# Loads of w_out in pieces of 64 columns, kept in that order on chip, and another room for its fifth load

## The chip, the cores and the metric

The kernel runs on one core of one Trainium2 chip. The metric is the device time of one execution in microseconds (us); lower is better. TensorE does the matrix products, VectorE (DVE), ScalarE (ACT) and GpSimd (POOL) the elementwise work, and SyncE (SP) mostly issues transfers. Each engine works through a queue of its own in order; transfers issued by SP and by ACT run on the same 16 DMA engines.

## The reference

Attention with a causal mask and a bias from a running sum, on 8 batches of 8 heads, 576 positions and 64 values per head, followed by a gated feed-forward layer on the 4608 x 512 result:

```python
scores = scale * np.matmul(q, k.transpose(0, 1, 3, 2))
cum = np.cumsum(np.maximum(s, 0.0), axis=-1)
bias = -(cum[:, :, :, None] - cum[:, :, None, :])
scores = np.where(causal, -1e9, scores + np.minimum(bias, 0.0))
attn = softmax(scores)                       # exp(scores - max) / sum
x = np.matmul(attn, v)                       # 8,8,576,64 -> 4608 x 512
gate = 1.0 / (1.0 + np.exp(-(x @ w_gate)))   # 512 x 1536
out = (gate * (x @ w_val)) @ w_out           # 1536 x 512
```

q, k, v, s are float32; the three weights are float64.

## The kernel before

**Precision.** Operands of the large products are split into a high and a low float16 part, and three products (high x high, high x low, low x high) are summed. The float64 weights arrive as pairs of 32-bit words and are turned into float32 on the chip (`decode_weight`: one ACT pass, line 270, and three DVE passes, lines 271 to 273), then scaled and split (`split_weight`: ACT at lines 286 and 291, a sum over partitions on POOL at line 288, DVE at line 292).

**Weight steps.** There are 18 steps, worked through by `weight_step` in order. Steps 0 to 11 bring a block of 128 columns of w_gate and w_val each. Steps 12 to 17 bring 256 rows of w_out each, 1 MB of float64 (two row blocks f and f+1 of 128 rows; a partition gets one row of each, 8 KB). `room(n)` names the place where the raw words of step n land (`raw`), the place of its float32 values (`dec`), and the step that must have been worked before the load may be issued. For the six w_out steps these stand in `outroom`. All six share the one float32 place `dec[0]` (tile `wa`). `raw[0]` is tile `ws`; `raw[1]` to `raw[3]` lie in the still unused parts of `w2all`; `raw[4]` and `raw[5]` lie in `t2big` (tile `t2f`), which later holds intermediate results of feed-forward units 8 to 15 and 16 to 23. At the start of step n, `weight_step` issues each outstanding load whose last step is below n. The loads of steps 12 and 13 are issued apart from that, at ticks 22 and 30 of the main loop. So the fifth w_out load (step 16) is issued at the start of step 15 into the room of step 14, and the sixth (step 17) at the start of step 17 into the room of step 16.

**Transfers of w_out.** `load_weight` splits a w_out load into two transfers on ACT's queue (lines 251 and 258), by halves of the 512 columns: 256 columns of both row blocks each, which are runs of 256 float64 (2 KB). `w2all[:, f]` then holds the 512 columns of the high part of row block f in one run, and those of the low part after it.

**Attention.** The first 8 heads (batch 0) are computed in float32; from head 8 on q, k and the probabilities are split into float16 parts and turned round by transposing transfers on SP's queue: `T<-qk` (line 394), `pt<-p` (line 493), `x<-x` (line 528). `swap_k` copies between partition halves (`T<-T`, lines 399 and 400) so that the second product of each score (line 446) can follow the first (line 445). `load_qk` (line 346) brings q and k of two heads in runs of 64 float32.

**Feed-forward.** The 4608 rows are cut into groups of 256. A unit (g, f) is one group and one of the 12 blocks of 128 hidden columns. `ffn_in` does 24 products with 256 columns each (line 656), `ffn_out` three per 128 rows with 512 columns of w_out as the moving operand (line 686, 1296 in all). The 24 units of the first two groups keep their result in `t2first` until all weight steps are done: `hidden_scale` needs the scales of all of them, and only after it do the products of line 686 begin. Weight steps 13 to 17 are emitted ahead of unit 12. A scheduler orders each engine's queue by priority with a simulated timeline.

Of the kernel before, what the change touches and what calls it, by code (L numbers as in the profile page):

```python
# [7 lines left out]
F16 = mybir.dt.float16  # L8
F32 = mybir.dt.float32
F32R = mybir.dt.float32r  # L10
I32 = mybir.dt.int32
# [5 lines left out]
P = 128  # L17
# [6 lines left out]
def tile_attention_then_gated_ffn(  # L24
# [13 lines left out]
    NT, DM = out.shape  # L38
# [4 lines left out]
    NF = DFF // P  # L43
# [13 lines left out]
    cp = ctx.enter_context(tc.tile_pool(name="cp", bufs=1))  # L57
# [10 lines left out]


    w1 = [cp.tile([P, NC, 2, 2, P], F16, name=f"w1_{f}") for f in range(NF)]  # L70
    w2all = cp.tile([P, NF, 2, DM], F16, name="w2all")
    w2 = [w2all[:, f] for f in range(NF)]
    e_s = [cp.tile([P, n * P], F32, name=f"e_{i}") for i, (_, _, n) in enumerate(SETS)]
    p_s = [cp.tile([P, 2, n * P], F16, name=f"p16_{i}") for i, (_, _, n) in enumerate(SETS)]

# [45 lines left out]
    def pow2_of(dst, ss, tag):  # L121

        e = wp.tile([P, 1], I32, tag="xe", name=f"xe_{tag}")
        nc.vector.tensor_scalar(e, ss.bitcast(I32), 1, 0x3F800000, ALU.logical_shift_right, ALU.bitwise_and)
        n = dst.shape[1]
        nc.vector.tensor_scalar(dst.bitcast(I32), e.to_broadcast([P, n]) if n > 1 else e, -1.0, 204.0 * 2.0 ** 23,
                                ALU.mult, ALU.add)
# [83 lines left out]

    raw0 = lp.tile([P, 8 * P, 2], I32, name="ws0")
    dec0 = lp.tile([P, 8 * P], I32, name="wa0")
    flat = w2all.rearrange("p f l n -> p (f l n)").bitcast(I32)
    raw = [raw0] + [flat[:, i * 16 * P : (i + 1) * 16 * P].rearrange("p (n t) -> p n t", t=2) for i in range(2)]
    dec = [dec0] + [flat[:, i * 8 * P : (i + 1) * 8 * P] for i in range(4, 6)]

# [3 lines left out]

    for i in (1, 2):
        raw.append(t2big[:, 8 * i * GT : 8 * (i + 1) * GT].bitcast(I32).rearrange("p (n t) -> p n t", t=2))
    outroom = [(4, 0, 0), (5, 0, 0), (0, 0, NF - 3), (3, 0, NF - 1), (0, 0, NF + 2), (0, 0, NF + 4)]

    def room(n):

        o, f = wsteps[n]
        if o == 0:
            return raw[f % 3], dec[f % 3], n - 3  # L230
        i, j, last = outroom[f // 2]
        return raw[i], dec[j], last

    def load_weight(n):
        o, f = wsteps[n]
        fs = slice(f * P, (f + 1) * P)
        r, d, _ = room(n)
        for x, src in enumerate((w_out,) if o else (w_gate, w_val)):
            src = src[f * P : (f + 2) * P, :] if o else src[:, fs]
            if wide:  # L240
                src = src.bitcast(I32)
                dst = r.rearrange("p n t -> p (n t)")
            else:
                dst = d.bitcast(F32)
            if o == 0:
                src = src.rearrange("(c p) n -> p c n", p=P)
                dst = dst.rearrange("p (c x n) -> p c x n", c=NC, x=2)[:, :, x]
            else:
                src = src.rearrange("(x p) (h n) -> h p x n", p=P, h=2)
                dst = dst.rearrange("p (x h n) -> h p x n", x=2, h=2)  # L250
                ins = nc.scalar.dma_start(dst[0], src[0])
                if n < NF + 2:
                    tc.keep_in_program_order(ins)
                src, dst = src[1], dst[1]
            if n < 2:
                nc.sync.dma_start(dst, src)
            else:
                ins = nc.scalar.dma_start(dst, src)
                if n == 2 or NF <= n < NF + 2:
                    tc.keep_in_program_order(ins)  # L260

    def decode_weight(n):

        o, f = wsteps[n]
        r, a, _ = room(n)
        if not wide:
            return a.bitcast(F32)
        m = w2all[:, f : f + 2].rearrange("p f l n -> p (f l n)") if o else w1[f].rearrange("p c g l n -> p (c g l n)")
        m = m.bitcast(I32)
        nc.scalar.activation(a.bitcast(F32), r[:, :, 1].bitcast(F32), AF.Copy, scale=2.0 ** -112)  # L270
        nc.vector.tensor_scalar(m, a, 3, 0x7FFFFFF8, ALU.logical_shift_left, ALU.bitwise_and)
        nc.vector.scalar_tensor_tensor(a, a, -0x80000000, m, ALU.bitwise_and, ALU.bitwise_or)
        nc.vector.scalar_tensor_tensor(a, r[:, :, 0], 29, a, ALU.logical_shift_right, ALU.bitwise_or)
        return a.bitcast(F32)

    def split_weight(n, a):

        o, f = wsteps[n]
        if o:
            a = a.rearrange("p (x n) -> p x n", x=2)  # L280
            hi, lo = w2all[:, f : f + 2, 0], w2all[:, f : f + 2, 1]
        else:
            a = a.rearrange("p (c n) -> p c n", n=P)
            hi, lo = (w1[f].rearrange("p c g l n -> p (c g) l n")[:, :, l] for l in range(2))
        ss = wp.tile([P, 1], F32, tag="wss", name=f"wss{n}")
        nc.scalar.activation(hi, a, AF.Square, accum_out=ss)
        tot = wp.tile([P, 1], F32, tag="wst", name=f"wtot{n}")
        nc.gpsimd.partition_all_reduce(tot, ss, P, ADD_REDUCE)
        pow2_of(wscale[:, o, f : f + 1 + o], tot, f"w{n}")
        sc = wscale[:, o, f : f + 1]  # L290
        nc.scalar.activation(hi, a, AF.Copy, scale=sc)
        nc.vector.scalar_tensor_tensor(lo, a, sc, hi, ALU.mult, ALU.subtract)
# [26 lines left out]
    def weight_step():  # L319
        n = wnext["step"]  # L320
        while n and wnext["load"] < len(wsteps) and room(wnext["load"])[2] < n:
            if not NF <= wnext["load"] < NF + 2:
                load_weight(wnext["load"])
            wnext["load"] += 1
        split_weight(n, decode_weight(n))
        wnext["step"] = n + 1
# [387 lines left out]
    for wnext["load"] in range(2):  # L714
        load_weight(wnext["load"])
# [13 lines left out]
    for n in range(nticks + 12):  # L729
# [13 lines left out]
        if 2 <= n < nticks + 2:  # L743
            a, z = divmod(n - 2, NTL)
# [5 lines left out]
        if 1 <= n < nticks + 1:  # L750
            a, z = divmod(n - 1, NTL)
# [7 lines left out]
        if 3 <= n < 3 + NTL * NN:  # L759
            with first():  # L760
                a, z = divmod(n - 3, NTL)
# [11 lines left out]
        if i < NH:  # L773
            p, j = divmod(i, 2)
            b, h = divmod(i, H)
# [80 lines left out]
            elif b == 1:  # L856
                if VSQ <= n < VSQ + vch:
                    v_square(2, n - VSQ)
                if VSQ + 5 <= n < VSQ + 5 + vch:
                    c = VSQ + 4 + vch - n  # L860
# [10 lines left out]
            if n in OUT:  # L871
                load_weight(NF + OUT.index(n))
# [3 lines left out]
        if n >= NE and state["u"] < 2 * NF:  # L876
            fdone = min(NF, int((n - NE + 1) * FPT))
            while state["u"] < 2 * fdone:
                f = state["u"]
# [17 lines left out]
        m = n - (11 if n > 2 * NTL * H + 30 else 7)  # L897
# [40 lines left out]
```

## Time and profile before

| | |
|---|---|
| runs | 1159.92, 1164.59, 1169.75 us (median 1164.59) |
| profiled execution | 1161.21 us, span 1159.4 us |
| mean granted TensorE clock | 0.979 |
| PE, PEld, DVE, ACT, POOL busy | 94%, 74%, 67%, 65%, 23% of the span |
| DMA queue of SP (q1) | 418398 packets, 127.12 MB |
| DMA queue of ACT (q10) | 13824 packets, 16.78 MB |

PE is the matrix product, PEld the loading of its stationary operand. Busy time of PE is counted from pipelined instructions, so a PE shown busy is not at its peak. A wait is put down to the event that came last. Names with an arrow are read as destination and source.

### The profile page before, as it was taken

How to read it: one execution, taken by the hardware profiler on the slowest of the kernel's cores; microseconds unless marked ns; L12 is line 12 of the kernel's file. 1: busy time of each engine (PE TensorE's matmuls, PEld its weight loads, DVE VectorE, ACT ScalarE, POOL GpSimd, SP SyncE). 2: the span in 40 equal slices, each digit the busy share in tenths (PEclk: the TensorE clock that was granted, in tenths of full speed). 3: DMA queues.
4: the chain of work that ended last, by engine and by line, in shares of the span. 5: the costliest groups of instructions: out<-in, count | busy, mean ns of one | idle time of the engine just before them, and what ended most of it. 6: DMA issues, size and time to landing. Idle time of an engine off the chain costs nothing.

```text
span 1159.4 us, 30337 instructions
## 1 busy us (share of the span) xinstructions
PE 1095.0 (94%) x11644; PEld 855.9 (74%) x11644; DVE 775.0 (67%) x2393; ACT 749.2 (65%) x1465; POOL 264.9 (23%) x570
## 2 busy tenths in 40 slices
PE   6786789989999999999999999999999999999997
PEld 5664677656777887778777777778877887787775
DVE  6888879785788777776566577777777775222221
ACT  6988667776777877676656577667777764233222
POOL 5535333231222222121111122222222221000000
PEclk9879899999999999999999999999999999999999
DMA  9675678898889797886737578877877764000000
GB/s 276 199 223 141 129 152 167 177 186 160 154 164 193 151 187 157 153 160 115 164 66 150 99 159 167 168 152 164 154 160 145 146 122 88 12 20 19 1 19 19
DMA packets 435886, 157.62 MB, mean 136 GB/s; under 512 B 403551, under 2 KB 423007, under 8 KB 435742
## 3 DMA queue, kind: packets, MB, share of 16 engines
q1 hardware_dynamic: 418398, 127.12, 57.1%
q10 hardware_dynamic: 13824, 16.78, 4.6%
q0 software_dynamic: 3520, 11.80, 3.1%
q8 instruction: 91, 1.49, 0.5%
q14 instruction: 53, 0.43, 0.1%
HBM read 56.92 MB, written 9.58 MB: 57 GB/s over the span
## 4 chain that ended last, share of the span: by engine, by line
PE 60%; issue 23%; DMA 5%; DVE 4%; ACT 3%; POOL 3%; SPq 1%; ACTq 0%; POOLq 0%; DVEq 0%
PE gv L656 33%; PE o L686 16%; PE s L446 3%; PE s L445 3%; DMA pt<-p 1%; PE av L505 1%; PE av L507 1%; PE av L506 1%; DMA T<-T 1%; POOL rl L460 1%; DMA T<-qk 1%; POOL cr L460 1%; PE na_ps L604 1%; DVE e L470 1%; DMA nqk<-in_q_dram 1%
## 5 line engine op out<-in xcount | busy, mean ns | idle before, releaser
L656 PE MATMUL gv<-x,w 128*128 128x256 f16 (+3 forms) x6912 | 614.9, 247 | 3.9 <-DVE t2f L663 2.3
L656 PEld LDWEIGHTS <-w 128*128 128x128 f16 x6912 | 535.1, 98 | 61.4 <-issue 4.6
L686 PE MATMUL o<-w2all,h 128*128 128x512 f16 x1296 | 314.8, 379 | 0.0
L460 POOL TENSOR_SCALAR_AFFINE_SELECT rl<-rl 128x64 f32<-128x64 f32 (+1 forms) x280 | 113.7, 407 | 512.0 <-DVE em L470 453.3
L473 ACT ACTIVATE e<-e,em 128x576 f32<-128x576 f32 x280 | 154.4, 554 | 88.0 <-DVE em L470 85.9
L661 ACT ACTIVATE th<-gv,scb 128x256 f32<-128x256 f32 (+3 forms) x288 | 111.3, 411 | 147.5 <-PE gv L656 142.5
L686 PEld LDWEIGHTS <-h 128*128 128x128 f16 x1296 | 123.4, 98 | 106.4
L663 DVE SCALAR_TENSOR_TENSOR t<-th,gv 128x256 f32<-128x256 f32 x192 | 80.0, 417 | 133.1 <-ACT th L661 131.9
L470 DVE CUSTOM_DVE_ANT_0 e<-s,rl,qkcf 128x288 f32<-128x288 f32 x280 | 135.7, 485 | 32.1 <-PE s L446 27.8
L671 ACT ACTIVATE h<-t,hsc 128x256 f16<-128x256 f32 x192 | 96.6, 503 | 80.4 <-DVE t L663 80.3
L482 DVE SCALAR_TENSOR_TENSOR p<-e,p 128x384 f16<-128x384 f32 x224 | 102.6, 498 | 41.0 <-ACT p L477 40.2
L672 DVE SCALAR_TENSOR_TENSOR h<-t,hsc,h 128x256 f16<-128x256 f32 x192 | 93.3, 486 | 43.4 <-ACT h L671 42.6
L477 ACT ACTIVATE p<-e 128x1152 f16<-128x1152 f32 x112 | 112.0, 1000 | 2.5
L505 PE MATMUL av<-v,pt 128*128 128x65 f16 x560 | 67.8, 193 | 5.3 <-DMA pt<-p 5.3
L446 PE MATMUL s<-T 128*128 128x288 f16 (+2 forms) x246 | 62.1, 279 | 11.3 <-DMA T<-T 11.3
L445 PE MATMUL s<-T 128*128 128x288 f16 (+2 forms) x246 | 64.4, 279 | 7.1 <-DMA T<-qk 4.2
L694 POOL DMA_DIRECT2D out_dram<-osb x36 | 20.4, 566 | 211.5 <-ACT osb L693 210.9
L507 PE MATMUL av<-v,pt 128*128 128x65 f16 x560 | 67.8, 194 | 0.0
L506 PE MATMUL av<-v,pt 128*128 128x64 f16 x560 | 67.7, 192 | 0.0
L505 PEld LDWEIGHTS <-pt 128*128 128x128 f16 x560 | 52.5, 98 | 11.0 <-DMA pt<-p 6.1
L408 POOL PARTITION_BROADCAST cr<-cr x63 | 58.5, 929 | 2.1 <-DMA cr<-cum_d 2.0
L506 PEld LDWEIGHTS <-pt 128*128 128x128 f16 x560 | 52.5, 97 | 4.9
(155 smaller groups left out, 1415.0 us busy)
## 6 DMA issues: line engine op xcount, KB each, us to landing
out_dram<-osb POOLq DMA_DIRECT2D x36, 256.0 KB, 2.8
v<-v SPq DMA_DIRECT2D x56, 162.5 KB
v<-in_v_dram SPq DMA_DIRECT2D x64, 128.0 KB
T<-T SPq DMA_DIRECT2D x82, 72.0 KB
t2f<-in_v_dram SPq DMA_DIRECT2D x20, 288.0 KB
qk<-in_q_dram SPq DMA_DIRECT2D x17, 288.0 KB
qk<-in_k_dram SPq DMA_DIRECT2D x17, 288.0 KB
w2all<-in_moe_w_gate_dram ACTq DMA_DIRECT2D x7, 512.0 KB
```

Source lines behind the costliest of these rows:

```text
L445: nc.tensor.matmul(ps[:, : b_ - a], lhs, T[i][:, 0, a:b_], start=True, stop=False)
L446: nc.tensor.matmul(ps[:, : b_ - a], lhs, T[i][:, 2, a:b_], start=False, stop=True)
L460: nc.gpsimd.affine_select(rl[i][:, q0:w], rl[i][:, q0:w], pattern=[[-1, m]], compare_op=ALU.is_ge, fill=-MASKED if i < NN else MASKED, bas ...
L470: nc.vector.tensor_tensor_reduce(e_t[t][:, a:b_], ps[:, : b_ - a], rl[i][:, a:b_], c, init, ALU.add, ALU.min, acc)
L473: nc.scalar.activation(e_t[t][:, :w], e_t[t][:, :w], AF.Exp, bias=init, scale=-1.0)
L477: nc.scalar.activation(p_s[h_][:, 0], e_s[h_], AF.Copy, scale=PSCALE)
L482: nc.vector.scalar_tensor_tensor(flat[:, LOW[t] * P : (LOW[t] + t) * P], e_t[t][:, : t * P], PSCALE, flat[:, kb * P : (kb + t) * P], ALU.m ...
L505: nc.tensor.matmul(AV[i][:, t], hi, v_[:, D : 2 * D + 1], start=kb == 0, stop=False)
L506: nc.tensor.matmul(AV[i][:, t, 0:D], hi, v_[:, 0:D], start=False, stop=False)
L656: nc.tensor.matmul(ps[:, gv, a:e], w1[f][:, cc, gv, wl], x_of(b, cc)[:, xl, c0 + a : c0 + e], start=(c == 0), stop=(c == 3 * NC - 1))
L661: nc.scalar.activation(th[:, a:e], ps[:, 0, a:e], AF.Tanh, scale=scb[b][:, f : f + 1])
L686: nc.tensor.matmul(ps[:m], h[:, hl, tt * P : tt * P + m], w2[f][:, wl], start=(f == 0 and c == 0), stop=(f == NF - 1 and c == 2))
```

## The change

It has two parts. First, a w_out load is split into its two transfers by row blocks instead of column halves, and each transfer is cut into pieces of 64 columns (512 bytes of float64), so that on chip the two row blocks alternate in pieces of 64 columns. That order is kept through decoding and splitting: `w2all` gets the shape [128, 6, 2, 8, 2, 64] (pair of blocks, high or low, piece, row block, column), and the moving operand of line 686 is read as 8 runs of 64 float16 (128 bytes) that lie 256 bytes apart. The bytes that each step occupies stay the same. Second, step 16 lands in `raw[5]` (the room of step 13) once step 13 has been worked, and step 17 in `raw[0]` once step 14 has been worked.

```diff
-    w2all = cp.tile([P, NF, 2, DM], F16, name="w2all")
-    w2 = [w2all[:, f] for f in range(NF)]
+    w2all = cp.tile([P, NF // 2, 2, 8, 2, DM // 8], F16, name="w2all")
+    w2 = [w2all[:, f // 2, :, :, f % 2] for f in range(NF)]
...
-    flat = w2all.rearrange("p f l n -> p (f l n)").bitcast(I32)
+    flat = w2all.rearrange("p f l h x n -> p (f l h x n)").bitcast(I32)
...
-    outroom = [(4, 0, 0), (5, 0, 0), (0, 0, NF - 3), (3, 0, NF - 1), (0, 0, NF + 2), (0, 0, NF + 4)]
+    outroom = [(4, 0, 0), (5, 0, 0), (0, 0, NF - 3), (3, 0, NF - 1), (5, 0, NF + 1), (0, 0, NF + 2)]
...
             else:
-                src = src.rearrange("(x p) (h n) -> h p x n", p=P, h=2)
-                dst = dst.rearrange("p (x h n) -> h p x n", x=2, h=2)
+                src = src.rearrange("(x p) (h n) -> x p h n", p=P, h=8)
+                dst = dst.rearrange("p (h x n) -> x p h n", x=2, h=8)
                 ins = nc.scalar.dma_start(dst[0], src[0])
...
-        m = w2all[:, f : f + 2].rearrange("p f l n -> p (f l n)") if o else w1[f].rearrange("p c g l n -> p (c g l n)")
+        m = w2all[:, f // 2].rearrange("p l h x n -> p (l h x n)") if o else w1[f].rearrange("p c g l n -> p (c g l n)")
...
         if o:
-            a = a.rearrange("p (x n) -> p x n", x=2)
-            hi, lo = w2all[:, f : f + 2, 0], w2all[:, f : f + 2, 1]
+            hi, lo = (w2all[:, f // 2, l].rearrange("p h x n -> p (h x n)") for l in range(2))
```

## The prediction

> **What bounds the kernel now.** I read the table by stretches first, because the page's 94% for PE is a mean over stages that differ, then PE's waits between 105 and 262 us, then the timelines around the w_out loads.
>
> ```profile
> core 0: us, PE busy (x) PEld busy (x) DVE busy (x) ACT busy (x) POOL busy (x), PEclk, DMA share, GB/s
> 105.00:118.00 13.00, 5.71 (x45) 4.79 (x45) 8.59 (x26) 9.07 (x16) 3.41 (x6) 0.88 0.80 155
> 118.00:156.00 38.00, 29.25 (x274) 24.15 (x273) 31.77 (x93) 27.26 (x47) 13.27 (x21) 0.90 0.70 149
> 156.00:190.00 34.00, 30.52 (x324) 25.79 (x322) 27.87 (x81) 23.24 (x41) 9.22 (x20) 0.95 0.77 152
> 190.00:215.00 25.00, 23.53 (x250) 19.60 (x248) 21.61 (x70) 17.90 (x36) 5.52 (x9) 1.00 0.81 159
> 262.00:1155.00 893.00, 885.17 (x9963) 693.78 (x9962) 560.23 (x1779) 545.79 (x1085) 160.83 (x379) 1.00 0.62 122
> ```
>
> From 262 us on PE is busy for 885.17 of 893 us: the rest of the kernel is PE's work, and no change of loads shortens it. What can move is PE's idle time before that. The w_out loads and their steps lie between 80 and 203 us (rows below); from 105 to 190 us PE idles 85 - 65.48 = 19.5 us. Its waits:
>
> ```profile
> PE s L446 <- DMA T<-T: 9.9, 5, 6.7
> PE av L505 <- DMA pt<-p: 5.3, 4, 3.9
> ```
>
> So the largest waits (total, times, longest) are for small transfers on SP's queue. The two longest of all fall directly behind a 1 MB load of w_out:
>
> ```profile
> 111.33 0.58 SPq L400 DMA_DIRECT2D T<-T  x1
> 110.81 0.39 ACTq L251 DMA_DIRECT2D w2all<-in_moe_w_out_dram  x1
> 117.76 0.42 PE L446 MATMUL s<-T 128*128 128x288 f16 x1 [6.70 <-DMA T<-T]
> 246.54 3.15 DMA T<-T
> 145.90 1.74 SPq L493 DMA_TRANSPOSE pt<-p  x1
> 146.39 0.37 ACTq L251 DMA_DIRECT2D ws<-in_moe_w_out_dram  x1
> 155.57 0.20 PE L505 MATMUL av<-v,pt 128*128 128x65 f16 x1 [3.88 <-DMA pt<-p]
> ```
>
> The swap of 111.33 landed 6.4 us later, where the chain shows 3.15 us for one with no w_out load beside it (246.54): some 3.3 us are the load's. After both waits the clock drops:
>
> ```profile
> 115.00:116.00 1.00, 0.00 (x0) 0.00 (x0) 0.00 (x0) 0.06 (x1) 0.00 (x0) 0.50 0.95 328
> 156.00:160.00 4.00, 4.00 (x32) 3.06 (x30) 1.46 (x7) 1.51 (x5) 0.54 (x3) 0.59 0.24 60
> ```
>
> (In such a row stand the stretch, its length, busy time and instructions of each engine, the clock, the DMA share and GB/s.) Behind the first wait PE still runs at 0.50 at 120 us (a row further down), behind the second at 0.59 on average for 4 us; if the gaps were short enough to keep the clock, up to 2 us more would be won in each place. Both prices are full only if nothing else is late there.
>
> **The products of line 686.** 1296 of them read w_out as 8 runs of 64 columns in place of one of 512. No row shows such a read, so I bound it.
>
> ```profile
> L686 PE MATMUL o<-w2all,h x1296: 377/379/382, 213.4 to 1152.5; 128*128 128x512 f16 x186
> 226.58 2.97 PE L686 MATMUL o<-w2all,h 128*128 128x512 f16 x13
> 141.75 0.19 PE L505 MATMUL av<-v,pt 128*128 128x65 f16 x1
> ...
> 142.93 0.20 PE L510 MATMUL av<-v,pt 128*128 128x64 f16 x1
> ```
>
> Thirteen in 2.97 us, the last lasting 0.379, start (2.97 - 0.379) / 12 = 0.216 us apart. Paid as eight separate products of 64 or 65 columns they would cost 8 x 0.030 = 0.242 us (40 rows from 141.75 to 142.93, 39 steps). The upper end is then 1296 x 0.026 = +34 us; the lower end is 0, since 512 columns are streamed either way. The nearest rows for a broken read are ACT's in the weight steps:
>
> ```profile
> L270 ACT ACTIVATE w2all<-w2all x8: 1107/1146/1174, 13.5 to 90.1; 128x1024 f32<-128x1024 f32 x8
> L291 ACT ACTIVATE w2all<-wa,wscale x6: 1132/1136/1139, 109.3 to 202.9; 128x1024 f16<-128x1024 f32 x6
> ```
>
> Line 270 reads every second 32-bit word and takes 1146 ns; line 291 reads as many in one run and takes 1136. Even a step at each element costs this engine under 1%. I take 0 for PE, and for the new order of writes of lines 286 to 292.
>
> **The longer transfers.** A load is now 2048 pieces of 512 bytes instead of 512 of 2 KB. Three seconds in which the queues were full give a rate by size of piece: 2 KB (w_out alone), 1 KB (w_gate and w_val), 256 bytes (q and k, line 346):
>
> ```profile
> 95.00:96.00 1.00, 1.00 (x12) 1.00 (x12) 1.00 (x2) 1.00 (x2) 1.00 (x1) 1.00 1.03 395
> 42.00:43.00 1.00, 1.00 (x13) 1.00 (x11) 0.87 (x4) 1.00 (x3) 1.00 (x4) 1.00 1.05 385
> 120.00:121.00 1.00, 1.00 (x7) 1.00 (x7) 0.17 (x1) 0.00 (x0) 0.00 (x0) 0.50 1.28 289
> L251 ACTq DMA_DIRECT2D ws<-in_moe_w_out_dram x3: 374/374/375, 80.3 to 181.9; - x3
> L251 ACTq DMA_DIRECT2D t2f<-in_moe_w_out_dram x2: 374/391/408, 84.1 to 92.5; - x2
> PE s L574 <- DVE em L583: 3.5, 4, 1.0
> ```
>
> 1.05 MB takes 2.65 us at 395 and 3.63 at 289; between 385 and 289, by time per piece on 16 engines (42.5 ns for 1 KB, 14.2 for 256 bytes, so 23.6 for 512), it is 347 GB/s or 3.0 us. So each load is +0.35 us, from 0 to +1.0. That is paid only where PE waits beside a load: at 117.76, and at 155.57, where after the change the sixth load lies (below). I add +0.35 twice. The loads of steps 12 to 14, issued between 80.3 and 92.5 us, lie beside float32 attention, where PE's longest waits are for DVE (line 574); 0 there, and +1.05 if that cover is gone.
>
> [...]
>
> **The moved loads.** Step 16's load waits for step 13's last read of `raw[5]`, step 17's for step 14's last read of `raw[0]`:
>
> ```profile
> 126.25 1.22 DVE L273 SCALAR_TENSOR_TENSOR wa<-t2f,wa 128x1024 int32<-128x1024 int32 x1
> 145.14 1.21 DVE L273 SCALAR_TENSOR_TENSOR wa<-ws,wa 128x1024 int32<-128x1024 int32 x1
> 187.55 1.28 DVE L292 SCALAR_TENSOR_TENSOR w2all<-wa,wscale,w2all 128x1024 f16<-128x1024 f32 x1
> 189.82 1.14 ACT L270 ACTIVATE wa<-ws 128x1024 f32<-128x1024 f32 x1
> 127.00:128.00 1.00, 1.00 (x12) 0.96 (x11) 0.81 (x2) 1.00 (x3) 0.62 (x1) 1.00 0.00 0
> 141.31 0.61 PE L445 MATMUL s<-T 128*128 128x288 f16 x3 [1.87 <-DMA T<-qk]
> 179.85 3.17 DMA T<-T
> 188.00:189.00 1.00, 0.80 (x6) 0.35 (x5) 1.00 (x2) 1.00 (x2) 0.00 (x0) 1.00 1.28 285
> 189.00:190.00 1.00, 0.83 (x9) 0.70 (x8) 1.00 (x4) 1.00 (x3) 0.43 (x1) 1.00 1.28 288
> ```
>
> So the load of 146.39 moves to 127.5 and that of 181.9 to 146.4: the collision at 146 stays, with another load in it. At 127.5 the DMA engines are idle, and the load is over by 132, before the next PE wait for a transfer at 141.31: 0, and +1.9 (as much again) if the transposes in between are pushed back. Behind the waiting issue on ACT's queue stands step 13's line 286, which waits for the same DVE instruction, as it did at 146.38; no new stall. The two issues of a load already stand on ACT's queue and are only moved; SP's and POOL's queues hold nothing of it.
>
> At 182 us a load goes away. The swap before it (179.85) was not slowed: 3.17 us in the chain. Only what PE idles between 188 and 190, 0.37 us, may be the load's, through a transpose and the q and k loads; I take -0.4, from -1.2 to 0.
>
> The old sixth load had to wait for step 16. That looks like a stall of several us, but step 17's first instruction began at 189.82, 1.0 us after step 16's line 292 ended at 188.83, and it could not begin earlier: both use the one `wa`. The chain of steps 13 to 17 is set by that place and by what else ACT and DVE do, not by the loads. So step 17 gains 1.0 us at most; the first product of line 686 needs its scale, and until 215 PE idles 1.47 us of 25. I take -0.5, from -1.0 to 0.
>
> **The sum.** 0 + 0.35 + 0.35 + 0 - 0.4 - 0.5 = -0.2 us: 1161.0 against the 1161.2 of the profiled execution (its span of 1159.4 with 1.8 us around it). That execution was 3.4 us under the median of 1164.59, so the forecast for a median is **1164.4 us**. The runs shown spread by 10 us; less than 1%, 11.6 us, is about what a measurement of this kernel can't tell from no change.
>
> **Rivals.**
>
> *The finer pieces let SP's small transfers pass.* If the DMA engines take turns piece by piece, a swap has less to wait for each turn. At 117.76 up to 3.3 us and 2 us of slow clock go, at 155.57 up to 3.9 and 2: -5 to -11, with the moved loads about 1155. For it: both long waits lie behind loads. Against it: the swap of 111.33 landed as late as if the whole 2.65 us load went first, so turns by piece are not what the rows show. [...] The 3.3 us here also speak against a swap passing after one packet.
>
> *PE pays for the broken read.* The place is line 686, the price up to 0.026 us a product; it decides from 9 ns a product (11.6 us / 1296), a little over 1 ns a run. All of it lands on the end, as PE is full from 262 us: +12 to +34, about 1182. Against it stand ACT's rows. [...]
>
> *The new load and another order cost more than they bring.* The load at 127.5 pushes the transposes back, the longer loads take their upper ends, and the scheduler puts other instructions first: 1.9 + 2.0 + some us, +4 to +10, about 1170.
>
> *The fifth and sixth load do not start earlier* (another wait holds them): then only +0.7 is left, inside the forecast.
>
> **Chances.** No change within 4 us: 0.57; small transfers pass: 0.20; the broken read costs: 0.10; new order costs: 0.13. For a range that leaves out 2 in 10 I drop the lower half of the first rival and nearly all of the second: **1153 to 1176 us**; the likeliest case alone is 1160 to 1169. Faster by over 1%: 0.11 (half of the first rival, a little of the rest); slower by over 1%: 0.11 (the second rival and the end of the third); within 1%: 0.78.
>
> **What would show it.** Line 686 still 379 ns each and 0.216 us apart; a changed spacing there makes the prediction wrong at once, and no other step can. Loads at about 127.5 and 146.4 in the timeline of ACT's queue, none near 182. A swap beside the load at 110.8 still near 6.4 us (under 4 would be the first rival). PE still idle for 3 to 4 us near 155. The first product of line 686 within 1 us of its old 213.4. PE's idle time after 262 us unchanged at some 8 us.

## The result, and the profile after

| | before | after |
|---|---|---|
| median | 1165.94 us (16 runs, 1159.92 to 1173.36) | 1156.88 us (16 runs, 1153.92 to 1162.45) |
| ratio | | 0.9925, 95% interval 0.9901 to 0.9948 |
| profiled execution | 1161.21 us | 1154.36 us |

The changed kernel is 0.75% faster, some 9 us. The time lies inside the predicted range and inside "within 1%", but the forecast was no change (1164.4 us, likeliest 1160 to 1169), and the interval leaves no room for that. The granted clock is not the gain: its mean is 0.979 in both profiled executions, 0.9775 over the 16 executions of after, and 0.977 over the 98 executions of before that were run beside the experiments. All line numbers from here on are those of the kernel after, one or two higher than before (line 686 is now 687, 446 is 447).

The same stretches as in the prediction, after (columns as there):

```profile
105.00:118.00 13.00, 9.76 (x62) 8.11 (x61) 10.97 (x26) 10.92 (x21) 4.64 (x8) 0.81 0.62 131
118.00:156.00 38.00, 33.52 (x312) 27.73 (x313) 33.10 (x93) 27.50 (x47) 9.76 (x22) 0.88 0.84 183
156.00:190.00 34.00, 28.21 (x310) 24.01 (x309) 32.19 (x104) 27.86 (x52) 12.33 (x22) 1.00 0.70 147
190.00:215.00 25.00, 24.33 (x242) 17.65 (x241) 22.48 (x79) 21.46 (x45) 9.17 (x16) 1.00 0.98 203
262.00:1155.00 893.00, 878.31 (x9902) 689.25 (x9900) 555.86 (x1766) 541.56 (x1077) 160.88 (x379) 1.00 0.61 121
```

PE is busy for 43.28 us between 105 and 156, where it was 34.96. Behind 262 us it has 6.9 us less to do (878.31 against 885.17), with 61 products fewer: the whole gain of the profiled execution (6.85 us) is made before 262. From the list of PE's waits between 105 and 262 us (total, times, longest):

```profile
PE av L506 <- DMA pt<-p: 7.5, 4, 3.2
PE na_ps L605 <- ACT p L597: 2.8, 2, 2.1
...
PE s L447 <- DMA T<-T: 0.7, 1, 0.7
```

The waits for the swapped scores have fallen from 9.9 us to 0.7, and the one of 6.7 us is gone. Those for `pt<-p` have not: 7.5 us in total instead of 5.3, the longest 3.2 instead of 3.9. PE's timeline around 118 us shows how:

```profile
116.85 1.03 PE L446 MATMUL s<-T 128*128 128x288 f16 x3 [0.31 <-DMA T<-qk]
117.68 1.81 PE L605 MATMUL na_ps<-v,p 128*128 128x65 f32 x8
119.28 0.84 PE L596 MATMUL nt_ps<-ident,e 128*128 128x128 f32 x3
119.92 1.38 PE L605 MATMUL na_ps<-v,p 128*128 128x65 f32 x6
121.10 1.06 PE L447 MATMUL s<-T 128*128 128x288 f16 x3
```

Before, the second score product stood directly behind the first on PE's queue and float32 products of batch 0 stood behind both, so PE sat out the swap. Now those products stand between the two, and the swap lands while they run. Nothing in the diff says so: **the queue has another order**. The scheduler simulates a timeline, and with transfers of another shape it ordered all five engines' queues anew (on PE's from 83 us to 318 us; behind that the two orders are the same). The weight steps moved with it. From the view by line of the kernel after (count, durations, first and last start): ACT's first instruction of a step, its split, and PE's products of line 687:

```profile
L272 ACT ACTIVATE wa<-ws x6: 1112/1136/1186, 10.9 to 170.7; 128x1024 f32<-128x1024 f32 x6
L292 ACT ACTIVATE w2all<-wa,wscale x6: 1133/1140/1148, 108.6 to 183.6; 128x1024 f16<-128x1024 f32 x6
L687 PE MATMUL o<-w2all,h x1296: 378/379/380, 191.7 to 1145.6; 128*128 128x512 f16 x186
```

Step 17 begins 19 us earlier than before (170.7 against 189.8), the last split is issued at 183.6 instead of 202.9, and the first line-687 product 21.7 us earlier. The groups of PE's feed-forward products in the first 262 us (busy time, mean ns), after:

```profile
L687 PE MATMUL o<-w2all,h 128*128 128x512 f16 x124 | 28.8, 379 | 0.0
L657 PE MATMUL gv<-x,w 128*128 128x192 f16 x36 | 4.3, 246 | 0.0
L657 PE MATMUL gv<-x,w 128*128 128x64 f16 x41 | 2.2, 193 | 0.0
```

and before:

```profile
L686 PE MATMUL o<-w2all,h 128*128 128x512 f16 x100 | 23.4, 379 | 0.0
L656 PE MATMUL gv<-x,w 128*128 128x192 f16 x17 | 2.1, 246 | 0.0
L656 PE MATMUL gv<-x,w 128*128 128x64 f16 x24 | 1.7, 193 | 0.0
```

By 262 us, 24 more of those products are issued (24 x 0.216 = 5.2 us of PE work) and 19 + 17 more of line 657 (with 0.216 / 512 = 0.42 ns a column an estimate of 2.0 us). That is 7.2 us of work done early, for 6.9 us gained. So I read the gain as feed-forward work that fills PE's waits while attention still runs, and the count of line-687 products issued before 262 us as its measure.

### The profile page after: what moved, and what is told of

Its sections match the earlier page's. It is cut to its first block, busy times and chain, and to the rows that moved or that the text cites. A ratio compares the mean times of both kernels' runs of the same rounds, so it can differ in the third digit from the quotient of the medians.

```text
span 1152.6 us, 30323 instructions
## 1 busy us (share of the span) xinstructions
PE 1098.2 (95%) x11644; PEld 859.3 (75%) x11644; DVE 776.1 (67%) x2393; ACT 747.9 (65%) x1465; POOL 263.2 (23%) x570
## 4 chain that ended last, share of the span: by engine, by line
PE 53%; issue 20%; POOL 2%; DMA 1%; DVE 1%; ACT 1%; SPq 0%; POOLq 0%; ACTq 0%; DVEq 0%
PE gv L657 29%; PE o L687 15%; PE s L447 2%; PE s L446 2%; PE av L508 1%; PE av L506 1%; PE av L507 1%; POOL rl L461 1%; PE av L510 1%; PE av L511 1%; DMA v<-in_v_dram 0%; POOL out_dram L695 0%; DMA t2f<-in_q_dram 0%; DMA t2f<-qk 0%; POOL cr L409 0%
## 5 line engine op out<-in xcount | busy, mean ns | idle before, releaser
L695 POOL DMA_DIRECT2D out_dram<-osb x36 | 20.4, 566 | 195.7 <-ACT osb L694 194.9
L506 PEld LDWEIGHTS <-pt 128*128 128x128 f16 x560 | 52.4, 97 | 14.3 <-DMA pt<-p 9.4
L409 POOL PARTITION_BROADCAST cr<-cr x63 | 56.1, 890 | 5.0 <-DMA cr<-cum_d 4.9
L455 DVE TENSOR_SCALAR rl<-cr,qkcf 128x576 f32<-128x576 f32 x56 | 29.1, 519 | 41.2 <-POOL cr L409 41.0
```

The costliest lines, as they stand in the source:

```text
L506: nc.tensor.matmul(AV[i][:, t], hi, v_[:, D : 2 * D + 1], start=kb == 0, stop=False)
```

## Experiments

**How the order was held.** After tracing, for each engine each instruction gets an edge to the one before it in a wanted list. The edges carry no semaphore: they bind the scheduler, not the chip.

```diff
+    _pin(tc)
...
+def _pin(tc):
+    ...
+    for names in order.values():            # one list per engine
+        for a, b in zip(names, names[1:]):
+            tc.add_manual_dep(traced[b], a, no_sync, reason="order kept")
```

"Old order" is the order that the scheduler made of the kernel before, "new order" that of the kernel after. Where the two kernels place the fifth and sixth w_out load differently, these four transfers are left free. Medians and ratios are against runs of the kernel before on the same chip; each run has 11 or 12 executions, x11 only 6. On PE's queue the traces of x1, x7 and x8 show the order of before, that of x2 the order of after, and that of x9 differs from before in one place.

| run | code | queues | ratio | 95% interval |
|---|---|---|---|---|
| x1 | after | old | 0.9978 | 0.9957 to 1.0000 |
| x2 | before | new | 0.9934 | 0.9910 to 0.9958 |
| x3 | pieces only | free | 0.9969 | 0.9950 to 0.9989 |
| x4 | rooms only | free | 1.0023 | 1.0002 to 1.0045 |
| x5 | before | new to 125 us, then old | 0.9978 | 0.9955 to 1.0002 |
| x6 | before | old to 125 us, then new | 1.0015 | 0.9991 to 1.0040 |
| x7 | pieces only | old | 0.9981 | 0.9956 to 1.0006 |
| x8 | rooms only | old | 0.9980 | 0.9956 to 1.0003 |
| x9 | before | old, one wait filled | 0.9997 | 0.9969 to 1.0024 |
| x10 | before | new to 191 us, then old | 0.9977 | 0.9956 to 0.9999 |
| x11 | before | new to 245 us, then old | 0.9922 | 0.9892 to 0.9951 |
| x12 | before | old to 213 us, then new | 1.0031 | 1.0001 to 1.0060 |

### Order or transfers: x1 and x2

x1 is the diff plus the pin with the old order; x2 is the kernel before plus the pin with the new order, not one line of the change in it.

> The changed kernel (finer pieces, both rooms) with every engine's queue pinned to the order that the scheduler wrote for the kernel before; only the two transfers each of the fifth and sixth w_out load take the places that the scheduler finds for them. Theory order (the gain comes from the order of the queues that the scheduler wrote anew, not from the transfers): ratio to before 0.997 to 1.003, PE's 6.7 us wait for a swap near 118 us still there within 1.5 us. Theory transfers (finer pieces and earlier loads make the small transfers land sooner): 0.990 to 0.996, with that wait cut below 4 us.

> The kernel before (2 KB runs, old rooms) with every engine's queue pinned to the order that the scheduler wrote for the changed kernel; the fifth and sixth w_out load alone find their own places, after the steps that free their old rooms. Theory order: 0.989 to 0.996, the wait near 118 us gone. Theory transfers: 0.997 to 1.003. A loss of the sixth load's early start should show as a later step 17, by at most some 5 us.

x1: 1161.49 us, x2: 1156.19 us (before 1164.75). The order alone, on unchanged code, brings 0.66%; the change alone, in the old order, about 0.2%, with an interval that touches 1. PE's wait in x1 is 5.0 us, a little less than the 5.2 that theory order allowed (x1's waits for the swap, then x2's):

```profile
PE s L447 <- DMA T<-T: 8.3, 5, 5.0
PE s L447 <- DMA T<-T: 1.0, 2, 0.9
```

In x2 the wait near 118 us is gone and the line-687 products come as early and as many as in the kernel after; nor is the last split later (183.0 us, 183.6 in after), so the sixth load's early start is not missed. From x2's views by line, the last one for the first 262 us:

```profile
L687 PE MATMUL o<-w2all,h x1296: 378/379/380, 191.1 to 1143.9; 128*128 128x512 f16 x186
L292 ACT ACTIVATE w2all<-wa,wscale x6: 1135/1144/1152, 107.1 to 183.0; 128x1024 f16<-128x1024 f32 x6
L687 PE MATMUL o<-w2all,h 128*128 128x512 f16 x129 | 30.0, 379 | 0.0
```

So the gain needs neither the pieces nor the rooms: here they served to make the scheduler find this order.

### Each part alone, queues free: x3 and x4

```diff
 x3: the pieces, with the old rooms
-    outroom = [..., (5, 0, NF + 1), (0, 0, NF + 2)]
+    outroom = [..., (0, 0, NF + 2), (0, 0, NF + 4)]
 x4: the rooms, with the old split of the load
-                src = src.rearrange("(x p) (h n) -> x p h n", p=P, h=8)
+                src = src.rearrange("(x p) (h n) -> h p x n", p=P, h=2)
```

> Finer pieces and the new layout of w_out alone, old rooms; the scheduler orders freely. Theory order: any ratio from 0.988 to 1.006, since the order is written anew, but the wait near 118 us (it lies ahead of the first moved load) as in the changed kernel, that is gone; most likely 0.992 to 0.997. Theory transfers: 0.992 to 0.998, the rest being the rooms'.

> The two new rooms alone, 2 KB runs and old layout; the scheduler orders freely. The order of all queues up to about 125 us is the same as before, so both theories expect the 6.7 us wait near 118 us to stay. Theory order: 0.996 to 1.004, with the last weight step up to 5 us earlier. Theory transfers: 0.995 to 1.000.

x3: 1160.56 us, x4: 1166.95 us. The pieces alone find an order that is better than the old one but not as good (102 line-687 products before 262 us); the rooms alone find a slightly worse one, in which the swap's wait stays (6.8 us) and the products begin at 220.6 us. Its last split is issued at 210.8 us, 8 us later than before and not up to 5 us earlier as expected. Two small edits, one gain and one loss, together the largest gain: no sum of parts, but three orders.

### Each part alone, in the old order: x7 and x8

> Pieces of 64 columns alone, the rooms of before, every queue in the order of before. If finer pieces let the small transfers of the SP queue pass sooner: the swap beside the fourth load lands in about 5 us instead of 6.4, the wait near 118 shrinks from 6.7 to about 5 us, ratio 0.9965 to 0.9995. If transfers of either shape cost the same (the prediction's terms, +0.35 and +0.35 us): ratio 0.9995 to 1.001.

> The fifth and sixth load in their new rooms, pieces of 256 columns as before, every other instruction in the order of before. The prediction's terms (load gone at 182: -0.4; step 17 earlier: -0.5 us): ratio 0.999. If the rooms are what costs in the run with rooms alone (1.0023): 1.001 to 1.004; if that was its order: 0.998 to 1.0005.

x7: 1161.19 us, x8: 1162.67 us (before 1165.4). Here only the transfers differ, and the swap that stands beside the fourth load can be compared. First its issue on SP's queue, then the product that waits for it; x7, then x8:

```profile
112.58 0.58 SPq L401 DMA_DIRECT2D T<-T  x1
117.58 0.42 PE L447 MATMUL s<-T 128*128 128x288 f16 x1 [5.26 <-DMA T<-T]
```

```profile
112.48 0.58 SPq L401 DMA_DIRECT2D T<-T  x1
119.87 0.42 PE L447 MATMUL s<-T 128*128 128x288 f16 x1 [7.65 <-DMA T<-T]
```

5.0 us from issue to use beside pieces of 512 bytes, 7.4 beside pieces of 2 KB. In x1 (512 bytes) it was 4.8; before 6.4, and in x4, x6 and x12 (2 KB) 6.3 to 6.8. So beside the load in finer pieces the swap was usable 1.3 us or more sooner, as the first expectation had it.

That the DMA engines take turns at smaller pieces does not follow. A swap is two transfers of 72 KB (64 packets of 1152 bytes each), issued 0.6 us apart, and in these seven runs the load's first issue comes 0.07 to 0.08 us behind the swap's first. The DMA packets in their traces show what came first:

| | 2 KB: before, x4, x6, x8, x12 | 512 bytes: x1, x7 | 2 KB: x9 |
|---|---|---|---|
| load's first packet behind its issue | 1.05 to 1.07 us | 1.52 and 1.53 us | 1.08 us |
| of the load's 1024 KB, started ahead of the swap's first transfer | 320 to 430 KB | none | none |
| ... ahead of its second transfer | 834 to 942 KB | 450 and 340 KB | 432 KB |
| second transfer's last packet behind its issue | 5.4 to 6.4 us | 3.8 and 4.1 us | 4.0 us |

In finer pieces the load starts later (1.52 and 1.53 us behind its issue, against 1.05 to 1.07), and the first half of the swap slips in ahead of it. x9 (below) has pieces of 2 KB, but there the load is issued 0.64 us behind the swap's first transfer and 0.06 behind its second; the first half slips in as well, and the second is as quick as in x1 and x7 (4.0 us against 3.8 and 4.1). So these eight runs show a race that is decided by tenths of a microsecond (0.07 or 0.64 us between the two issues, some 1.06 or 1.52 us to the load's first packet); a gain from turns by smaller pieces is not shown.

In time the pieces are worth at most what x7 shows, -0.2%, and that interval holds 1. So does that of x8 (0.9980), but it lies below the 1.001 to 1.004 expected if the rooms were what cost in x4: it was x4's order. No run pins the old order with nothing else changed, so whether these -0.2% belong to the transfers or to the pin is open; x9, which is the old order but for one place, has 0.9997 (0.9969 to 1.0024) and gives no sign that the pin itself gains.

### Which part of the order: x5 and x6, x9 to x12

x5, x6, x10, x11 and x12 hold one order up to an instruction and the other behind it. x9 moves one thing in the old order:

```diff
 PE's queue in x9 (instructions 321 to 355 of it)
-  5 score products (the first waits for the swap), 11 float32 products,
-  4 score products, 6 float32 products
+  17 float32 products, then all 9 score products
```

> The code of before; its engines' queues in the order of after up to the last float32 product (about 125 us into the span) and in the order of before behind it. Theory A (the gain is the wait for the swapped scores near 118 us, 6.7 us long, behind which ready float32 products stood): that wait is gone, the first line-687 product comes 4 to 8 us before 213, ratio 0.993 to 0.997. Theory B (the gain is made later, by weight steps 14 to 17 that stand earlier in the queues): ratio 0.998 to 1.002, whether or not the wait near 118 goes.

> The code of before; its queues in the order of before up to the last float32 product and in the order of after behind it. Theory A (the wait near 118 us is the gain): the wait of 6 to 7 us is still there, ratio 0.997 to 1.002. Theory B (weight steps 14 to 17 earlier in the queues): the last split of the weights ends near 190 instead of 203, the first line-687 product comes near 200, ratio 0.993 to 0.997.

> Code and queues of before, but for one place of TensorE's queue: 17 float32 products of the native attention, which stood behind the score product that waits 6.7 us near 118 us, stand ahead of it (about 3.5 us of work). If the wait costs as much as work is kept behind it (theory A): ratio 0.996 to 0.998, the wait down to 3 to 4 us. If a filled wait is given back at the next waits of this stage, as in the run with the new order up to 125 us: 0.9985 to 1.001.

x5: 1162.37 us, x6: 1165.26 us (before 1165.4), x9: 1165.97 us (before 1164.94). Neither theory holds alone. In x5 the wait near 118 us is gone, and of the 4 to 8 us that theory A gave it 2 to 3 are left, with an interval that touches 1. The first line-687 product comes at 218.5 us, but in an execution 4.9 us above x5's median, so that it is later than before is not shown; that it is 4 to 8 us earlier neither. In x6 the wait of 7.0 us stays, yet the last split is issued at 195.7 and the first line-687 product at 203.8 us, ten earlier than before, and the time is that of before. That earlier weights alone are worth nothing does not quite follow, for PE also waits 4.7 us in x6 where after and x2 have 1.6 for the same:

```profile
PE nx_ps L629 <- DVE nx L615: 4.7, 1, 4.7
```

In x9 the long wait is gone from PE's list:

```profile
PE av L506 <- DMA pt<-p: 6.5, 3, 3.5
PE s L446 <- DMA T<-qk: 4.0, 3, 1.9
PE s L446 <- DVE em L471: 3.8, 7, 1.2
PE s L447 <- DMA T<-T: 2.8, 3, 1.5
```

and the time is that of before: a filled wait alone is worth nothing that this comparison can see either. This profiled execution, 3.4 us above its median, was late from the start: the score product of 110.77 us begins at 117.27. Between 80 and 100 us its granted clock was 0.69, where before it was 0.91 (x9, then before):

```profile
80.00:100.00 20.00, 16.60 (x67) 11.41 (x68) 12.43 (x39) 16.17 (x32) 6.93 (x12) 0.69 0.73 223
80.00:100.00 20.00, 14.38 (x77) 9.67 (x74) 16.13 (x50) 18.25 (x35) 11.19 (x17) 0.91 0.74 239
```

On PE's queue, instruction by instruction, it is 6.5 us behind before at that product, 0.4 to 2.5 us behind from the filled wait until 184 us, and 3.6 us behind at 188.0 us, after a wait of 2.6 us for `pt`. So in this execution the filled wait did pay where it stood, and at least part of it was waited away at a later place.

> The code of before; all queues in the order of after up to the first line-687 product (about 191 us), in the order of before behind it. If the gain lies ahead of that place (the wait near 118 filled, and what was pulled forward behind it, weight steps 14 to 17 with it): ratio 0.992 to 0.996. If the order has to be new to its end, and every crossing from one order to the other costs some us: 0.997 to 1.001.

> The code of before; all queues in the order of after up to the transpose of the eighth block of x (about 245 us), in the order of before behind it. If the gain lies ahead of 245 us: ratio 0.992 to 0.996, as with the whole order of after (0.9934). If it needs the new order behind that too: 0.996 to 1.0.

> The code of before; all queues in the order of before up to the first line-687 product (about 213 us), in the order of after behind it. If the gain lies ahead of that place: ratio 0.998 to 1.003, the wait of 6 to 7 us near 118 still there. If it lies behind it: 0.993 to 0.997.

x10: 1163.70 us, x11: 1155.95 us, x12: 1167.81 us (before 1164.94). x11 has the whole gain, x10 under a third of it; they differ in what stands on the queues between 191 and 245 us. From x10, the stretch from 191 to 215 us, PE's wait in it, and the view by line:

```profile
191.00:215.00 24.00, 19.41 (x194) 15.78 (x193) 17.06 (x60) 16.25 (x35) 4.09 (x10) 0.86 0.71 147
```

```profile
PE s L446 <- DVE em L471: 4.5, 3, 2.4
```

```profile
L292 ACT ACTIVATE w2all<-wa,wscale x6: 1133/1136/1148, 111.3 to 189.2; 128x1024 f16<-128x1024 f32 x6
L687 PE MATMUL o<-w2all,h x1296: 377/379/382, 218.2 to 1157.9; 128*128 128x512 f16 x186
```

From x11, the same stretch, the group of line 687 in it, and the last split:

```profile
191.00:215.00 24.00, 23.11 (x229) 16.49 (x227) 21.46 (x74) 19.56 (x41) 8.78 (x15) 1.00 0.95 196
```

```profile
L687 PE MATMUL o<-w2all,h 128*128 128x512 f16 x39 | 8.9, 379 | 0.0
```

```profile
L292 ACT ACTIVATE w2all<-wa,wscale x6: 1134/1136/1149, 107.0 to 184.7; 128x1024 f16<-128x1024 f32 x6
```

In both w_out is split by about 190 us. By the count of PE's products done, x10's execution is 5.5 us behind that of after at 184 us and 11.9 behind at 242 us. There the old order has the hidden values and the line-687 products behind 215 us all the same, and PE stands 4.5 us behind score products that wait for DVE (line 471). In x11 39 line-687 products fill that stretch, and PE idles 0.9 us of 24.

x12 shows the other side: the order behind 213 us on an old beginning gains nothing. So in these runs the gain comes only where three things stand together: the wait near 118 filled, the weight steps pulled forward into the time won, and line-687 products placed among attention's from 191 on. Without the first (x6, which the other wait of 4.7 us makes less sure), without the third (x10) or with the first alone (x5, x9) most or all of it is missing; no run has the first and the third without the second. Over all fourteen profiled executions, line-687 products issued before 262 us stand beside the time of that same execution:

| | x2 | x11 | after | x1 | x7 | x3 | before | x8 | x10 | x12 | x6 | x9 | x5 | x4 |
|---|---|---|---|---|---|---|---|---|---|---|---|---|---|---|
| products | 129 | 126 | 124 | 104 | 104 | 102 | 100 | 96 | 95 | 93 | 85 | 83 | 81 | 75 |
| us | 1152.7 | 1155.1 | 1154.4 | 1161.6 | 1159.7 | 1159.5 | 1161.2 | 1166.7 | 1166.7 | 1164.4 | 1165.3 | 1169.4 | 1167.3 | 1169.5 |

From 129 to 75 products, 16.8 us: 0.31 us each, where one is 0.216 us of PE work; the rest is other work done early. The count shows where an execution stands at 262 us, not why; why is what the cut orders show. It also holds what differs between executions of one kernel: those of x4, x5, x8, x9 and x10 lie 2.5 to 4.9 us above the medians of their runs, those of before, x2 and x12 over 3 us below, and x5, x9 and x10 were 3 to 5 us late by 97 us, ahead of any place where their order was cut. What stays open is the price of a cut itself: instructions on either side of it stand in an order that no scheduler weighed, and x12 (1.0031, 3.6 us) lets it be some us. The sizes of x5, x6, x10 and x12 hold that price too; x2 and x11, which gain in full, do not need it.

## Why the prediction was right and wrong

**The time was inside the range, the reason given for it was not what happened.** That is luck: the range reached down to 1153 us for the sake of the first rival, and the gain came another way. The failed step is the one that was never argued: that instructions stay where they are on the queues and only durations change. The prediction names a new order once, in the third rival, as "some us" more; it was some 8 us less (x2). Every term of the sum was read at places (117.76, 155.57, 182, 189.82) that the new order has moved or filled. (The "three seconds" of the rates by size of piece are three stretches of 1 us.)

By its own list of what would show it:

- *Line 687 at 379 ns, 0.216 us apart:* right. 20 products in 4.48 us are (4.48 - 0.379) / 19 = 0.216 us apart:

```profile
191.70 4.48 PE L687 MATMUL o<-w2all,h 128*128 128x512 f16 x20
```

  Eight runs of 128 bytes cost the moving operand nothing in this kernel (13 products in 2.97 us, 0.216 us apart, before), so the rival with 12 to 34 us falls.
- *Loads at 127.5 and 146.4:* they came earlier, none near 182:

```profile
119.43 0.55 ACTq L253 DMA_DIRECT2D t2f<-in_moe_w_out_dram  x1
132.78 0.55 ACTq L253 DMA_DIRECT2D ws<-in_moe_w_out_dram  x1
```

  In the old order (x1) they stood at 126.4 and 147.2: the step was right for an unchanged queue.
- *The swap beside the load at 110.8 still near 6.4 us:* wrong, 4.8 and 5.0 (x1, x7). The two terms of +0.35 us took the load for a block whose length counts. They had the wrong sign: the swap came sooner. Nor is a longer load to be seen: the third w_out load, near 90 us, takes 3.6 to 4.5 us from first to last packet in 2 KB pieces and 3.6 to 4.4 in pieces of 512 bytes. The first rival was right in kind, but its reason, turns by piece, is not what the packets show; under 4 us, its mark, was not reached, and of its 5 to 11 us the runs in the old order show 2 to 3 (x1, x7), with intervals that hold none.
- *PE idle 3 to 4 us near 155:* wrong. From 131 to 200 us PE's longest wait in after is 2.1 us, and its longest for `pt` stands at 235:

```profile
178.64 0.20 PE L506 MATMUL av<-v,pt 128*128 128x65 f16 x1 [2.10 <-DMA pt<-p]
235.13 0.20 PE L506 MATMUL av<-v,pt 128*128 128x65 f16 x1 [3.19 <-DMA pt<-p]
```

- *The first line-687 product within 1 us of 213.4:* wrong, 191.7. The step said that the chain of weight steps 13 to 17 is set by the one `wa` and by "what else ACT and DVE do", and so could win 1.0 us. No run speaks against the first half; but what else ACT and DVE do is what the scheduler chose, and x2 has the chain 20 us earlier with the old loads.
- *Idle time behind 262 us:* as foretold. Of 893 us PE is idle for 14.7, but 9.0 of these lie behind its last product (1145.6 + 0.4 against 1155), where before it was 2.1 of 7.8: 5.7 us in both. (The stretch ends 2.4 us behind the end of after's span.)

The term for the load that goes at 182 (-0.4) and that for step 17 (-0.5) cannot be told from nothing in x8.

## What to carry to other kernels

Where a scheduler orders the queues from a simulated timeline, a change of a transfer's shape is two changes: what the transfer costs, and another order of everything; pin the old order to see the first and put the new order on the old code to see the second. On an engine that works in order, look first for ready work that stands behind a waiting instruction (before, 17 float32 products behind PE's wait of 6.7 us); but here filling one wait paid in the end only where independent work was also ready and queued at the next ones. A profile of before can only price places that will still be there.

## What the runs showed of the hardware

- A load of 1 MB on ACT's queue began to move 1.02 us after its issue at the earliest in pieces of 2 KB (x2, x11) and 1.34 us in pieces of 512 bytes (after, x3); the last load of before, in pieces of 2 KB, began 1.5 us behind its issue.
- A 72 KB swap issued 0.5 us behind such a load was usable 4.8 and 5.0 us after its issue beside pieces of 512 bytes (x1, x7), 6.3 to 7.4 us beside 2 KB (before, x4, x6, x8, x12); what differed was whether the transfer ahead of it on SP's queue got in before the load's first packet.
- The issue itself grew: 0.55 to 0.81 us on ACT's queue in after for half a load of 1024 pieces, 0.37 to 0.63 us before for one of 256; single ones took longer in other runs (0.91 us in x7, 1.07 in x2 with 256).
- Products with 512 float16 columns of moving operand stood 0.216 us apart read in 8 runs of 64 (after, 20 in 4.48 us) and in one run of 512 (before, 13 in 2.97 us), at 379 ns each in both.
